# Attention times a gated MLP on one core: the sums of x are split behind the product that frees their home, stores of q and k go one product later, a quarter of x is reloaded ahead of W tile 10, and the first row tiles and V's last group are reordered

## The chip, the core and the metric

The kernel runs on one core of one Trainium2 chip. The core has five engines that take their instructions in order, each from a list of its own: TensorE (PE; its weight loads are listed apart as PEld and overlap it), VectorE (DVE), ScalarE (ACT), GpSimd (POOL) and SyncE (SP). They wait for one another through semaphores. In this kernel SyncE does nothing but issue DMA transfers; ScalarE issues some as well, and in the profile the DMA issues of these two stand apart as SPq and ACTq. Data lies in DRAM, in SBUF (where instructions take most operands) and in PSUM (where TensorE writes its products).

The metric is the time of one execution on the device, in microseconds (us). The profile is that of one execution, with times counted from the start of its span; the median of several executions is given beside it.

## The reference

With one batch, S = 2048 rows, D = 1024 columns, 32 heads of 32 columns and an MLP width of 3584:

```python
def _A_ref(x, wqkv, wo):
    qkv = (x @ wqkv).reshape(B, S, 3, H, Dh).transpose(2, 0, 3, 1, 4)
    q, k, v = qkv[0], qkv[1], qkv[2]
    scores = jnp.einsum("bhqd,bhkd->bhqk", q, k) * (Dh ** -0.5)
    p = _softmax(scores, axis=-1)
    o = jnp.einsum("bhqk,bhkd->bhqd", p, v)
    return o.transpose(0, 2, 1, 3).reshape(B, S, D) @ wo

def _B_ref(x, w1, b1, w2):
    h = jnp.einsum("bsd,df->bsf", x, w1) + b1
    act = h * jnp.tanh(softplus(h))          # mish
    return jnp.einsum("bsf,fd->bsd", act, w2)

xn = _layernorm(x, axis=-1)
return x + _A_ref(xn, wqkv, wo) * _silu(_B_ref(xn, w1, b1, w2))
```

## The kernel before, in words

**Arithmetic.** Almost every matrix product is taken with operands that are split in two: a high part, which ScalarE makes with a copy to the type fp32r, and a low part, which VectorE or GpSimd makes by subtracting the high part from the original (`copy`, L288, and `low`, L296). A product then takes three matmuls: high by high, and the two of high by low (`THREE`). A *split* below is one such copy with its subtraction.

**Four stages.** First comes the layernorm with the product for V, then the products for q and k, then attention and the MLP side by side, then the output projection. The columns of x are its 2048 rows turned round: four chunks of 512, each in SBUF as two units of four row blocks, `xc0_0` to `xc3_1`. Each unit holds a high and a low part, so it has four times [2 x 128 x 512].

**Layernorm and V.** A loop goes over 16 row tiles of 128 rows. For one tile, VectorE takes the statistics (`ln_a`, in three steps: two halves and their combination), ScalarE the inverse root (`ln_r`), VectorE the offsets (`ln_b`), ScalarE normalises (`ln_x`; for tiles 0 to 2, VectorE takes one half of it), TensorE transposes it (`ln_t`, tiles `pt`) and ScalarE and VectorE split the result into the units (`ln_c`). In the same turn `v_group(0, t - 2)` multiplies a row tile, two behind, with the first half of V's weights, 24 matmuls. These weights come in as `vraw` and are split into four buffers of two row blocks each, `vw0_0` to `vw0_3` (`v_high` and `v_low`, written out one by one for the first tiles, L470 to L495). The order of the 24 matmuls inside a group is a parameter: by default row block by row block with all three products each (`THREE`), otherwise two of the three products over all row blocks and then the third. When the last row tile is through, the second half of V's weights is split (`v_split(1, j)`) into the buffers that the first half leaves, and 16 more groups follow (`v_group(1, t)`).

During these last 16 groups, sums and differences of units of x are also formed (`t_half`), for the scheme of the next stage. Those for the chunk pair (0, 1) have no place in SBUF yet and are stored to DRAM, unsplit, as `ts0` to `ts3`, [128 x 512] at a time.

**q and k.** The columns of W for q and k are 8 column tiles each, and a column tile of q is paired with that of k; the sixteen "tiles" q = 0 to 15 are these 8 pairs for the chunk pair (2, 3) and then the same 8 for the pair (0, 1). A pair of column tiles times a pair of chunks is a 2 x 2 block product, made with seven products instead of eight, i = 0 to 6: A11, S2, A12, S3, S1, A22, S4, named by what W contributes. W's contribution is a block of W itself or a sum or difference of blocks (`w_sum`, on GpSimd), split by `piece(n)` into half of a buffer `wq{n // 2}`. x's contribution is a unit or a stored sum; the list `X` says which SBUF unit holds it, its *home*. `product(n)` issues 12 matmuls into a PSUM bank; then `after()` adds it to the others (`e` tiles, L777) or, when a block of q or k is complete, calls `out_`, which splits it into a staging tile `qst` (a ring of four) and stores that to DRAM through ScalarE's queue. `later.at(t, f)` does f t products later.

`SEQ` lists the products in order; some of tile 7 and tile 8 are moved between those of the tile before (`EARLY`). Counted from (7, 0), the first product of tile 7 to be issued, the index `since` means: 0 (7,0), 1 (6,1), 2 (6,2), 3 (7,2), 4 (6,3), 5 (6,4), 6 (7,1), 7 (6,5), 8 (6,6), 9 (7,3), 10 (7,4), 11 (8,0), 12 (7,5), 13 (7,6), 14 (8,1), and then 15 to 19 are (8,2) to (8,6). Pieces are made for two products at once: `wq26` holds those of (7,3) and (7,4), `wq27` those of (8,0) and (7,5).

At this passage from tile 7 to tile 8, x's contributions change. The sums for the pair (0, 1) have to come back from DRAM and be split into homes that the pair (2, 3) leaves: `xc2_0` is free after (7,0), `xc2_1` after (7,2), `xc3_0` after (7,1), `xc1_0` after (7,3). `t_load(i, k)` loads [128 x 512] of sum i into one of five small buffers and asks for its split three products later; odd k go to GpSimd, even k to VectorE. There are 16 such loads, in the order of sums 1, 2, 0, 3. The last unit, B22 (row blocks 4 to 7 of chunk 1), also comes back from DRAM, already split, into `xc1_1`, which is free after (7,4); it takes four loads of 512 KB and is first wanted by (8,6), since = 19. At the same time raw column tiles of W are loaded: each tile has two halves of 512 KB, a ring of two tiles serves up to tile 9 (`raw0` to `raw3`), and from tile 10 on two more stand in `spare`, the SBUF that `xc3_1` leaves after (7,6). All of these loads are issued by SyncE, in the order in which the code is written.

**Attention and MLP.** Here a planner (`Plan`) simulates the engines with estimated costs and due times and writes the order of all instructions. The score product `t` of head 0 needs, in two rows of `qstack0`, the negated row maxima; those of the last four row tiles of head 0 are made by `m_chain(0, 12, 4, ...)`: a reduction, a split, a transposition by TensorE (`mtp0_12`), a copy to `mt0_12` by ScalarE and two small DMAs into `qstack0` (`r6`), issued by SyncE.

## Time and profile before

| | us |
|---|---|
| three runs | 3372.64, 3367.37, 3369.28 |
| their median | 3369.28 |
| the profiled execution | 3371.32 |
| its span | 3369.5 |
| TensorE busy in the span | 3344.0 |
| VectorE busy | 2510.7 |
| ScalarE busy | 2056.4 |
| GpSimd busy | 2526.6 |

The mean clock granted to TensorE in the span is 0.999 of full speed. TensorE takes its first product of q and k at 202 us and its last at 530 us; attention and the MLP fill most of the rest.

How to read the rows of the profile. A row of busy times gives microseconds, the share of the span and the number of instructions. A row of waits gives the engine, operation, output tile and code line, `<-` what it waited for, and then the total in us, the number of waits and the longest. A row of a timeline gives the start, the duration of the group (several instructions of one kind that follow each other), the engine, the code line, the operation, output `<-` inputs, shapes, the count, and in brackets the idle time ahead of it and what ended it. A row of windows gives a stretch of time A:B, its length, then the busy time of TensorE (with the number of its matmuls), of its weight loads, of VectorE, ScalarE and GpSimd, then TensorE's granted clock, the busy share of the 16 DMA engines and the GB/s that they moved; where nothing ran on an engine its column is empty. Engine names with a q are DMA issues. Tile numbers are left out in these rows, so that `xc<-t` stands for the split of any sum into any unit.

### The profile page before, as it was taken

What the parts mean: (1) busy time and instruction counts of PE and PEld (TensorE: products, weight loads), DVE (VectorE), ACT (ScalarE), POOL (GpSimd) and SP (SyncE); (2) the same over time, 40 slices, a digit from 0 to 9 for tenths busy, and PEclk for the clock granted to TensorE, in tenths of its full rate; (3) what the DMA queues carried; (4) which work ended last, traced back from release to release, by engine and by line L of the source; (5) the groups of instructions that cost most, each with busy time, mean ns of one, the idle gap of its engine ahead of it and who ended that gap; (6) DMA issues with size and microseconds to landing.
All of it is one profiled execution on the core that took longest, in us unless ns stands there. A gap on an engine that the chain in (4) does not pass through costs nothing.

```text
span 3369.5 us, 45748 instructions
## 1 busy us (share of the span) xinstructions
PE 3344.0 (99%) x16867; PEld 2455.6 (73%) x16867; DVE 2510.7 (75%) x3984; ACT 2056.4 (61%) x3314; POOL 2526.6 (75%) x751
## 2 busy tenths in 40 slices
PE   8999999999999999999999999999999999999999
PEld 7888787777777777777677767777677777767787
DVE  6665677878777777887788778888787888886542
ACT  5233335777766666676676766767667766667621
POOL 2332445999999977888888988888888898889800
PEclk9999999999999999999999999999999999999999
DMA  7864755455555643334335434333344433433482
GB/s 242 297 207 165 238 163 166 149 176 161 166 175 179 210 135 114 113 117 118 112 113 156 136 101 126 100 102 113 113 151 132 123 101 111 127 114 107 137 305 84
DMA packets 291460, 501.56 MB, mean 149 GB/s; under 512 B 88138, under 2 KB 151114, under 8 KB 269130
## 3 DMA queue, kind: packets, MB, share of 16 engines
q1 hardware_dynamic: 271524, 456.95, 43.6%
q10 hardware_dynamic: 19712, 41.69, 3.3%
q8 instruction: 133, 2.18, 0.3%
q14 instruction: 91, 0.75, 0.1%
HBM read 352.55 MB, written 144.97 MB: 148 GB/s over the span
## 4 chain that ended last, share of the span: by engine, by line
PE 87%; DMA 2%; DVE 1%; ACT 0%; issue 0%; SPq 0%; ACTq 0%; POOL 0%; DVEq 0%
PE y L1290 18%; PE h L1200 18%; PE t L995 14%; PE s L913 13%; PE pv L1042 13%; PE op L1389 5%; PE q_y L792 2%; PE q_x L792 1%; PE q_z L792 1%; PE zp L1068 1%; PE s L697 0%; DMA xc<-xs 0%; DMA raw<-in_A_wqkv_dram 0%; DMA qstack<-mt 0%; DMA w2r<-in_B_w_dram 0%
## 5 line engine op out<-in xcount | busy, mean ns | idle before, releaser
L1024 POOL TENSOR_TENSOR z<-z,p 128x2048 f32<-128x2048 f32 x448 | 2067.9, 4616 | 97.4 <-ACT p L285 72.3
L285 ACT ACTIVATE p<-t,zero 128x512 f32<-128x512 f32 x2048 | 1376.9, 690 | 559.6 <-PE t L995 535.4
L919 DVE TENSOR_REDUCE mx<-s 128x1 f32<-128x512 f32 x1984 | 1322.3, 685 | 383.1 <-PE s L913 372.1
L1290 PE MATMUL y<-w,act 128*128 128x512 f32 x2688 | 920.7, 391 | 0.8 <-DVE yacc L1312 0.5
L995 PE MATMUL t<-qstack,kstack 128*128 128x512 f32 x2048 | 799.0, 393 | 3.3 <-DMA qstack<-mt 2.3
L913 PE MATMUL s<-kstack,qstack 128*128 128x512 f32 x1984 | 772.5, 393 | 0.0
L1200 PE MATMUL h<-xr,w 128*128 128x512 f32 x2016 | 697.7, 391 | 0.2 <-DMA xr<-xs 0.2
L1290 PEld LDWEIGHTS y<-w,act 128*128 128x128 f32 x2688 | 503.3, 188 | 114.5 <-issue 6.7
L995 PEld LDWEIGHTS t<-qstack,kstack 128*128 128x128 f32 x2048 | 383.8, 188 | 118.0 <-issue 20.1
L1042 PE MATMUL pv<-p,v 128*32 128x512 f32 x4096 | 459.3, 594 | 0.0
L913 PEld LDWEIGHTS s<-kstack,qstack 128*128 128x128 f32 x1984 | 369.7, 188 | 118.0 <-issue 32.1
L1200 PEld LDWEIGHTS h<-xr,w 128*128 128x128 f32 x2016 | 378.3, 188 | 80.9 <-issue 3.4
L1312 DVE TENSOR_TENSOR yacc<-yacc,y 128x512 f32<-128x512 f32 x416 | 282.7, 680 | 82.3 <-PE y L1290 81.2
L1042 PEld LDWEIGHTS pv<-p,v 128*32 128x32 f32 x4096 | 123.3, 110 | 282.9 <-issue 281.2
L1024 POOL TENSOR_TENSOR z<-p,p 128x2048 f32<-128x2048 f32 x32 | 148.0, 4626 | 185.6 <-PE zp L1068 136.1
L1200 PE MATMUL h<-xc,w 128*128 128x512 f32 x672 | 231.3, 391 | 0.3 <-ACT p L285 0.3
L354 PE MATMUL v<-vw,xc 128*128 128x512 f32 x768 | 180.3, 393 | 0.9 <-DVE vw L296 0.7
L354 PEld LDWEIGHTS v<-vw,xc 128*128 128x128 f32 x768 | 143.1, 189 | 31.9 <-DVE vw L296 1.8
L1200 PEld LDWEIGHTS h<-xc,w 128*128 128x128 f32 x672 | 125.9, 188 | 29.3 <-issue 2.5
L288 ACT ACTIVATE act<-h 128x512 fp32r<-128x512 f32 x112 | 66.6, 595 | 87.2 <-DVE h L1249 86.0
L792 PE MATMUL q_y<-xc,wq 128*128 128x512 f32 x480 | 115.4, 389 | 0.5 <-DVE e L777 0.5
L792 PEld LDWEIGHTS q_y<-xc,wq 128*128 128x128 f32 x480 | 90.0, 188 | 19.7 <-ACT wq L288 0.9
(146 smaller groups left out, 2943.5 us busy)
## 6 DMA issues: line engine op xcount, KB each, us to landing
w<-w1s SPq DMA_DIRECT2D x91, 1024.0 KB
w<-w2s SPq DMA_DIRECT2D x168, 512.0 KB
w2s<-w SPq DMA_DIRECT2D x56, 512.0 KB
qstack<-qs SPq DMA_DIRECT2D x96, 256.0 KB
kstack<-ks SPq DMA_DIRECT2D x96, 256.0 KB
w1s<-w SPq DMA_DIRECT2D x21, 1024.0 KB
qs<-qst ACTq DMA_DIRECT2D x32, 512.0 KB
ks<-qst ACTq DMA_DIRECT2D x32, 512.0 KB
```

What stands on the lines that cost most here:

```text
L285: nc.scalar.activation(out_, in_, fn, bias=zero if bias is None else bias, scale=scale)
L354: nc.tensor.matmul(ps, xc[t // 4][k // HK][:, a, k % HK, (t % 4) * P:(t % 4 + 1) * P], vw[i, k // 2][:, b, k % 2], start=n == 0, stop=n == ...
L792: nc.tensor.matmul(ps, w[:, a, k], xx[:, b, k], start=m == 0 and i in (0, 1, 4), stop=m == 3 * HK - 1, skip_group_check=i not in (0, 1, 4))
L913: nc.tensor.matmul(sp_, qst[h % 3][:, qt * P:(qt + 1) * P], kst[h % 3][:, kc * 512:(kc + 1) * 512], start=True, stop=True)
L919: nc.vector.reduce_max(tiles["mx"][:, qt, kc:kc + 1], tiles[qt, kc], axis=AX.X)
L995: nc.tensor.matmul(tp, kst[h % 3][:, kt * P:(kt + 1) * P], qst[h % 3][:, c * 512:(c + 1) * 512], start=True, stop=True)
L1024: nc.gpsimd.tensor_tensor(zs[h], pts[T - 1] if kt == 1 else zs[h], pts[T], ALU.add)
L1042: nc.tensor.matmul(pv[h][c * DH:(c + 1) * DH, :], vt[h][:, k, :], pts[T - kt + k][:, c * 512:(c + 1) * 512], start=k == 0, stop=k == NT - 1)
L1200: nc.tensor.matmul(t["h"], w1t[n][:, a, k], xts_[c][k // HK][:, b, k % HK], start=i == 0, stop=i == 3 * KT - 1)
L1290: nc.tensor.matmul(t["y"], acts[n][:, p, s * P:(s + 1) * P], w2t[m_][:, q], start=j == 0 and i == 0, stop=j == YB - 1 and i == 2)
L1312: nc.vector.tensor_tensor(ya, ya, t["y"], ALU.add)
L1389: nc.tensor.matmul(ps[t, dh], ohl[t // 4, k][:, a, s * P:(s + 1) * P], wt[k][:, b, r], start=k == 0 and i == 0, stop=k == KT - 1 and i == 2)
```

## The change

It has six parts.

1. In the first row tiles, the second and third step of tile 1's statistics move ahead of the subtraction for row block 2 of V's weights, on VectorE.
2. V's last group of the first half (row tile 15) takes its matmuls row block by row block, all three products of one before the next, instead of two products over all row blocks and then the third.
3. The splits of x's sums are no longer tied to three products behind their load. They stand in a list, and `T_SPLITS` takes two from it at since = 1, 2, 4, 5, 7, 8, 10 and 11, which is the product behind the one that frees the home, or the second behind it. `T_LOADS` starts the loads at since = -2 instead of 0 and ends them at 8 instead of 11.
4. B22's four loads are issued in two pairs at since = 11 and 12 instead of one each at 12 to 15, and the two halves of W tile 9 at 6 and 9 instead of 9 and 11.
5. The store of a block of q or k comes four products after the one that completed it instead of three.
6. The two small DMAs of head 0's last row maxima are issued by ScalarE instead of SyncE.

```diff
@@ first row tiles
     ln_a(1, (0,))
     ln_c(0)
+    ln_a(1, (1, 2))
     v_low(0, 2, nc.vector)
     v_high(0, 3)
     v_low(0, 3, nc.vector)
     for k in (4, 5):
         v_high(0, k)
         v_low(0, k, nc.gpsimd)
-    ln_a(1, (1, 2))
@@ the loop over row tiles
         evac = v_group(0, t - 2, {2: 22, 3: 20, 4: 14}.get(t, 8), (lambda: ln_t(t - 1)) if t <= NT else None,
-                       (((0, 0), (1, 0)), ((0, 1),)) if t == 2 else (((0, 0), (0, 1)), ((1, 0),)))
+                       (((0, 0), (1, 0)), ((0, 1),)) if t == 2 else None if t > NT else (((0, 0), (0, 1)), ((1, 0),)))
@@ q and k
+    t_splits = []
+
     def t_load(i, k):
...
-        later.at(3, split)
+        t_splits.append(split)
...
-    T_COUNT = (2, 1, 1) * 4
-    B_COUNT = {12: (0,), 13: (1,), 14: (2,), 15: (3,)}
+    T_LOADS = {-2: 3, -1: 1, 0: 1, 1: 2, 2: 2, 4: 2, 5: 2, 7: 2, 8: 1}
+    T_SPLITS = {s: 2 for s in (1, 2, 4, 5, 7, 8, 10, 11)}
+    B_LOADS = {11: (0, 1), 12: (2, 3)}
...
-        later.at(3, lambda: move(dst, st, nc.scalar))
+        later.at(4, lambda: move(dst, st, nc.scalar))
...
         later.tick()
+        since = n - SEQ.index((KT - 1, 0))
+        for _ in range(T_SPLITS.get(since, 0)):
+            t_splits.pop(0)()
...
         after()
-        since = n - SEQ.index((KT - 1, 0))
-        if 0 <= since < len(T_COUNT):
-            for _ in range(T_COUNT[since]):
-                t_load(*T_ORDER.pop(0))
-        if since in (9, 11):
-            q_load(9, ring_of(9), (since == 11,))
-        for k in B_COUNT.get(since, ()):
+        for _ in range(T_LOADS.get(since, 0)):
+            t_load(*T_ORDER.pop(0))
+        if since in (6, 9):
+            q_load(9, ring_of(9), (since == 9,))
+        for k in B_LOADS.get(since, ()):
             move(X[1][6][:, :, k], xs[1][:, :, HK + k])
@@ m_chain
         def r6(at):
             for a in range(2):
                 move(qst[h % 3][96 + a:97 + a, first * P:(first + n) * P]
-                     .rearrange("o (t p) -> o t p", p=P), tiles["mt"][n * a:n * a + n, :])
+                     .rearrange("o (t p) -> o t p", p=P), tiles["mt"][n * a:n * a + n, :], None if h else nc.scalar)
```

The order of TensorE's instructions is that of before but for V's last group. The other engines' lists change at these places. In the rows, tiles carry a number that tells allocations apart.

SyncE's list at the passage from tile 7 to tile 8, before. `t3_*` are the last loads of x's sums, `raw2` and `raw3` the two halves of W tile 9, `xc1_1` is B22's home, and `spare` holds W tile 10.

```order
L745 DMA t3_0_3005<-ts3_139 128x512
L745 DMA t3_1_3007<-ts3_139 128x512
L543 DMA raw2_1897<-in_A_wqkv_dram 128x8x128
L745 DMA t3_2_3029<-ts3_139 128x512
L745 DMA t3_3_3057<-ts3_139 128x512
L543 DMA raw3_1898<-in_A_wqkv_dram 128x8x128
L292 DMA xc1_1_186<-xs1_141 128x2x512
L543 DMA spare_3095<-in_A_wqkv_dram 128x8x128
L292 DMA xc1_1_186<-xs1_141 128x2x512 x2
L543 DMA spare_3095<-in_A_wqkv_dram 128x8x128
L292 DMA xc1_1_186<-xs1_141 128x2x512
L543 DMA spare_3095<-in_A_wqkv_dram 128x8x128
```

The same place in SyncE's list after:

```order
L747 DMA t0_3_2918<-ts0_136 128x512
L747 DMA t3_0_2920<-ts3_139 128x512
L543 DMA raw2_1897<-in_A_wqkv_dram 128x8x128
L747 DMA t3_1_2969<-ts3_139 128x512
L747 DMA t3_2_2971<-ts3_139 128x512
L747 DMA t3_3_2992<-ts3_139 128x512
L543 DMA raw3_1898<-in_A_wqkv_dram 128x8x128
L292 DMA xc1_1_186<-xs1_141 128x2x512 x4
L543 DMA spare_3102<-in_A_wqkv_dram 128x8x128 x3
L292 DMA zeros_156<-qstack0_3308 32x2048
```

The four loads of B22 now stand in one block behind `raw3`, and the three halves of W tiles in `spare` behind them.

VectorE's list between the additions e7_1 and e7_3 (of the products (7,1) and (7,3)), before. `wq26` and `wq27` are the W buffers described above, a row `xc<-t` is the subtraction of a sum's split, `qst` that of a block of q or k for the store, and the rows of L777 add products.

```order
L777 TENSOR_TENSOR e7_1_2924<-q7_y_2905,e7_0_2779 128x512
L296 TENSOR_TENSOR wq26_2942<-ws3_2891,wq26_2942 128x512
L296 TENSOR_TENSOR wq26_2942<-ws4_2838,wq26_2942 128x512
L296 TENSOR_TENSOR xc2_1_188<-t2_2_2872,xc2_1_188 128x512
L296 TENSOR_TENSOR qst6_1_3_2902<-e6_3_2870,qst6_1_3_2902 128x512
L777 TENSOR_TENSOR q6_y_2785<-q6_y_2785,e6_0_2762 128x512
L777 TENSOR_TENSOR q6_z_2874<-q6_z_2874,e6_1_2804 128x512
L296 TENSOR_TENSOR wq27_2990<-raw0_1895,wq27_2990 128x512
L569 SCALAR_TENSOR_TENSOR wq27_2990<-raw3_1898,wq27_2990 128x512
L296 TENSOR_TENSOR xc3_0_189<-t0_0_2926,xc3_0_189 128x512
L296 TENSOR_TENSOR qst6_1_2_2955<-q6_y_2785,qst6_1_2_2955 128x512
L777 TENSOR_TENSOR e7_3_3003<-q7_y_2905,e7_0_2779 128x512
```

The same place after:

```order
L780 TENSOR_TENSOR e7_1_2937<-q7_y_2922,e7_0_2786 128x512
L296 TENSOR_TENSOR wq26_2952<-ws3_2905,wq26_2952 128x512
L296 TENSOR_TENSOR wq26_2952<-ws4_2856,wq26_2952 128x512
L296 TENSOR_TENSOR qst6_1_3_2917<-e6_3_2882,qst6_1_3_2917 128x512
L296 TENSOR_TENSOR xc3_0_189<-t0_0_2839,xc3_0_189 128x512
L780 TENSOR_TENSOR q6_y_2790<-q6_y_2790,e6_0_2767 128x512
L296 TENSOR_TENSOR xc3_0_189<-t0_2_2886,xc3_0_189 128x512
L780 TENSOR_TENSOR q6_z_2888<-q6_z_2888,e6_1_2813 128x512
L296 TENSOR_TENSOR wq27_3006<-raw0_1895,wq27_3006 128x512
L569 SCALAR_TENSOR_TENSOR wq27_3006<-raw3_1898,wq27_3006 128x512
L296 TENSOR_TENSOR qst6_1_2_2968<-q6_y_2790,qst6_1_2_2968 128x512
L780 TENSOR_TENSOR e7_3_3016<-q7_y_2922,e7_0_2786 128x512
```

Two subtractions of sum 0, `t0_0` and `t0_2`, now stand ahead of the split of `wq27`; before, one of sum 2 did, and one of sum 0 stood behind it.

ScalarE's list at the end of q and k before: `p0` and `p1` are the exponentials of the first score products, `hl` the copy for the split of the row maxima, `mt0_12` the transposed ones.

```order
L285 ACTIVATE p0_4492<-t0_2_4499,zero_160 128x512
L288 ACTIVATE hl_3317<-nm0_12_4502 128x4
L288 ACTIVATE mt0_12_4525<-mtp0_12_4521 8x128
L285 ACTIVATE p0_4492<-t0_3_4551,zero_160 128x512
L285 ACTIVATE p1_4563<-t1_0_4556,zero_160 128x512
```

After, two DMA issues stand in it:

```order
L285 ACTIVATE p0_4492<-t0_2_4499,zero_160 128x512
L288 ACTIVATE hl_3316<-nm0_12_4502 128x4
L288 ACTIVATE mt0_12_4525<-mtp0_12_4521 8x128
L292 DMA qstack0_3308<-mt0_12_4525 1x4x128 x2
L285 ACTIVATE p0_4492<-t0_3_4551,zero_160 128x512
L285 ACTIVATE p1_4563<-t1_0_4556,zero_160 128x512
```

They stand directly behind the copy that makes their data, and ahead of the exponential of `t0_3`.

## The prediction

> **What bounds the kernel now.** I read the page's busy times first, then TensorE's waits, then its timeline at each wait, and last the queues of the engines named there.
>
> ```profile
> span 3369.5 us, 45748 instructions
> PE 3344.0 (99%) x16867; PEld 2455.6 (73%) x16867; DVE 2510.7 (75%) x3984; ACT 2056.4 (61%) x3314; POOL 2526.6 (75%) x751
> PE pt L423 <- ACT x L285: 9.8, 2, 9.0
> PE q_z L792 <- DMA xc<-xs: 3.3, 1, 3.3
> PE t L995 <- DMA qstack<-mt: 2.3, 2, 1.7
> PE q_y L792 <- DVE e L777: 1.9, 2, 1.4
> PE v L354 <- DVE vw L296: 0.7, 1, 0.7
> ```
>
> TensorE is busy for 3344.0 of 3369.5 us, so only 25.5 us can be won by moving work about, and 9.0 of them are the wait for the first tile of x. Every part of this change lies ahead of 545 us, and the order of TensorE's instructions behind that is the same in both kernels. TensorE alone sets the time there, so what is won or lost early should arrive at the end undiminished. The five wait rows are five places; the change touches all of them.
>
> The largest is where the projection passes from its first pair of chunks (q tiles 0 to 7) to its second.
>
> ```profile
> 319.36:349.29 29.93, 29.93 (x134) 24.78 (x133) 17.88 (x25) 13.96 (x26) 15.52 (x11) 1.00 0.69 229
> 349.29:388.00 38.71, 33.54 (x134) 26.41 (x133) 25.86 (x35) 15.71 (x29) 14.59 (x11) 0.91 0.78 258
> 349.29 2.88 PE L792 MATMUL q_x<-xc,wq 128*128 128x512 f32 x12
> 353.58 3.00 PE L792 MATMUL q_y<-xr,wq 128*128 128x512 f32 x12 [1.41 <-DVE e L777]
> 361.86 2.98 PE L792 MATMUL q_x<-xc,wq 128*128 128x512 f32 x12
> 365.34 2.98 PE L792 MATMUL q_y<-xc,wq 128*128 128x512 f32 x12 [0.50 <-DVE e L777]
> 373.60 2.20 PE L792 MATMUL q_z<-xc,wq 128*128 128x512 f32 x9
> 379.06 1.65 PE L792 MATMUL q_z<-xc,wq 128*128 128x512 f32 x3 [3.26 <-DMA xc<-xs]
> 380.50 4.89 PE L792 MATMUL q_x<-xc,wq 128*128 128x512 f32 x12
> 379.00:385.00 6.00, 5.94 (x15) 0.52 0.17 62
> ```
>
> The first two rows hold 134 matmuls each, eleven products of 2.72 us (29.93 / 11); the second eleven take 38.71 us, which is 8.8 more. From 349.29 to 353.58 is 4.29 (1.6 over), from 361.86 to 365.34 is 3.48 (0.8 over). The remaining 6.4 belong to one event: 3.26 us of waiting for the last quarter of B22, and then, as the last row shows, a clock of 0.52, at which twelve matmuls took 4.89 instead of 2.88.
>
> **B22 ahead of W tile 10.** The loads stand on SyncE's queue.
>
> ```profile
> 356.06 3.21 SPq L292 DMA_DIRECT2D xc<-xs  x1
> 364.37 5.32 SPq L292 DMA_DIRECT2D xc<-xs  x1
> 364.37 14.64 DMA xc<-xs
> ```
>
> Before, the four loads are issued from 356.06 to 369.7 with three of W tile 10 between them, and the last lands 14.64 us after 364.37, at 379.0. After, the four stand together ahead of W tile 10. What they still follow on SyncE is the second half of W tile 9, whose buffer comes free when VectorE has split the W piece of product (7,5), the second half of wq27 (in the rows below the split at 348.75; about 352 in the reckoning there). So they are issued from 352 to 354, W tile 9 and B22 being 2.5 MB. At the 258 GB/s of the second row, half of it left to the stores on ScalarE's queue, that is 19 us; at the whole rate 10. They land between 362 and 371. B22's last quarter is wanted at 375.8 before (373.60 + 2.20), hence at about 371.5 once the delays ahead of it are taken out. The wait goes, and with it the slow clock: minus 6.4. Bounds: minus 6.4, and minus 3.2 if 19 us is right and the clock falls all the same. What is late next is VectorE.
>
> **The sums of x, and the stores.** VectorE was 25.86 us busy in the slow stretch against 17.88 ahead of it, and its lateness explains the waits of 1.41 and 0.50.
>
> ```profile
> 341.69 1.79 DVE L296 TENSOR_TENSOR wq<-ws,wq 128x512 fp32r<-128x512 f32 x2
> 343.56 1.67 POOL L551 TENSOR_TENSOR ws<-raw 128x512 f32<-128x512 f32 x1 [1.23 <-DVE wq L296]
> 345.70 0.68 DVE L777 TENSOR_TENSOR q_y<-q_y,e 128x512 f32<-128x512 f32 x1
> 346.27 0.63 ACT L288 ACTIVATE xc<-t 128x512 fp32r<-128x512 f32 x1 [4.01 <-issue]
> 347.94 0.89 DVE L296 TENSOR_TENSOR wq<-raw,wq 128x512 fp32r<-128x512 f32 x1 [0.95 <-ACT wq L288]
> 348.75 1.78 DVE L569 SCALAR_TENSOR_TENSOR wq<-raw,wq 128x512 fp32r<-128x512 f32 x1
> 352.76 0.67 DVE L777 TENSOR_TENSOR e<-q_y,e 128x512 f32<-128x512 f32 x1
> ```
>
> A VectorE operation with both inputs in SBUF takes 0.89 by itself (347.94) and up to 1.78 beside GpSimd; one that reads PSUM keeps 0.68 (345.70). The two take turns, some 1.7 us for one of each. The change does not remove any of the 16 splits (a copy on ScalarE, a subtraction on VectorE or GpSimd); it moves them two or three products earlier. The first four now fall at 324 to 328, where VectorE and GpSimd had been idle. The order rows say what then happens at 341 to 352: between e7_1 and e7_3 there stand ten operations on VectorE before and ten after, but after, two subtractions of x's sums (t0_0, t0_2) lie ahead of the split of wq27, where before one did (t2_2). I follow the queues by these durations, in turns wherever GpSimd has work: e7_1 ends at 341.3, wq26 is split by 343.2, qst6_1_3 by 343.9, t0_0 by 345.6, q_y by 346.2. ScalarE can then copy qst6_1_2, t0_2, t0_3 and both pieces of wq27 by 349.1, which lets VectorE do t0_2 by 348.6, q_z by 349.2, the first piece of wq27 by 350.3, the second by 352.0 and e7_3 by 353.2. TensorE wants the first of these pieces at its third matmul behind 349.29, at 349.75, and waits 0.6; it then wants e7_3 at 352.6 and waits 0.7. So I keep 1.3 of stall here and win 2.4 (1.6 and 0.8) minus 1.3, about 1.0. Bounds: 2.4 if turns are kinder, and a loss of 1.0 if they are harsher by one pair (1.7) at each of the two places. The second wait (0.50, at 365) goes, since two fewer subtractions are left by then.
>
> Stores a product later: no instruction more. ScalarE sat idle for 4.01 before 346.27 because a store in its queue waited for qst<-e; that block goes, but what stood behind it waited for q_y at 345.70 anyway, so it is worth 0.4 to VectorE and is in the reckoning above. In the other tiles of W TensorE shows no wait, and I cost it at nothing there; the cover is a staging ring of four, reused seven products later.
>
> **V's last group.**
>
> ```profile
> 104.69 13.72 PE L354 MATMUL v<-vw,xc 128*128 128x512 f32 x59
> 112.70 3.24 ACT L288 ACTIVATE vw<-vraw 128x512 fp32r<-128x512 f32 x6 [3.48 <-PE v L354]
> 119.13 33.09 PE L354 MATMUL v<-vw,xc 128*128 128x512 f32 x143 [0.72 <-DVE vw L296]
> ```
>
> The group of row tile 15 starts 16 matmuls (3.6 us) into the first row, at 108.3. Before, it reads its first W buffer until matmul 18 (112.4), and ScalarE's splits start at 112.70. After, it has done with it at matmul 6, 109.7: the splits start 2.7 us earlier, and the wait of 0.72 goes. Minus 0.7.
>
> **The first row tiles.**
>
> ```profile
> 12.24 2.39 DVE L296 TENSOR_TENSOR vw<-vraw,vw 128x512 fp32r<-128x512 f32 x2
> 12.72 3.07 POOL L296 TENSOR_TENSOR vw<-vraw,vw 128x512 fp32r<-128x512 f32 x2 [11.42 <-ACT vw L288]
> 15.59 0.74 DVE L296 TENSOR_TENSOR vw<-vraw,vw 128x512 fp32r<-128x512 f32 x1
> 18.06 1.10 PE L423 MATMUL pt<-ident_r,x 128*128 128x128 f32 x8 [0.85 <-ACT x L285]
> ```
>
> The statistics of tile 1 move ahead of two subtractions on VectorE, but its normalisation stays behind these and a third. VectorE has no idle time there. Before, the first of the three starts at 12.24 and is nearly through when GpSimd begins at 12.72, and the third ends at 16.3 (15.59 + 0.74). After, the first starts behind 12.72 too, so one more of 0.74 takes its turn between there and the end, which becomes 17.1. Normalising, and TensorE at 18.06, come later by up to 0.8; I take plus 0.6, bounds 0.8 and minus 0.3 (the statistics' own 1.0 less what overlaps).
>
> [...]
>
> **The row maxima of head 0 on ScalarE's queue.**
>
> ```profile
> 533.04 0.37 ACTq L292 DMA_DIRECT2D qs<-qst  x1
> 536.30 1.21 SPq L292 DMA_DIRECT2D qstack<-mt  x2
> 540.67 0.47 PE L995 MATMUL t<-qstack,kstack 128*128 128x512 f32 x1 [1.66 <-DMA qstack<-mt]
> DMA  8999999798996999999998889999996200000464
> ```
>
> The last row cuts 525 to 545 into slices of half a microsecond: the DMA engines are full until 540.5. The two small transfers gain nothing at their issue, since they follow ScalarE's copy in both kernels. But on ScalarE's queue they now stand behind the last stores of q and k, which themselves go later: one more store of 512 KB is still to be moved. At 305 to 410 GB/s (what the slices moved) that is 1.3 to 1.7 us. I take plus 1.2. Bounds: minus 0.4 if it makes no difference whose queue it is and SyncE's issue is saved, plus 4.6 if 1.7 makes the wait 3.3 long and the clock falls as it did after 3.26 (2.9 more: 6.4 minus 3.26, rounded down).
>
> [...]
>
> **Sum.** Minus 6.4, minus 1.0, minus 0.7, plus 0.6, plus 1.2: minus 6.3. The profiled execution took 3371.32 us, so 3365.0; the median of the three runs, 3369.28, is 2.0 below it, so 3363.0. A measurement of this kernel tells about 0.2% from no change, 6.7 us: the borders are 3362.5 and 3376.0, and the forecast lies next to the first.
>
> **Rivals.**
> *Everything goes clean* (0.23): VectorE is in time, the maxima are not delayed, the front neither. Minus 6.4, 2.4 and 0.7: minus 9.5, 3359.8. For it: the first four splits fall into idle time. Against: 16 splits and GpSimd's sums still share 30 us.
> *A slow clock in a new place* (0.20): one of the waits at 352 or 541 grows past 3.2 us, and 2.9 come back: minus 3.4, 3365.9. For it: 3.26 was enough at 376; the wait at 541 is reckoned at 2.9. Against: 1.66 and 1.41 were not.
> *B22 is hardly earlier* (0.08): it still waits for W tile 9's buffer; if VectorE frees that after 355, half of the 6.4 stays: minus 3.1, 3366.2.
> *Slower* (0.10): the 16 loads share five buffers, so a load waits for a split five earlier, and ScalarE, which takes its queue in order, holds back evacuations behind a copy whose load has not landed.
>
> ```profile
> 353.15 1.89 SPq L745 DMA_DIRECT2D t<-ts  x2
> 361.50 0.63 ACT L288 ACTIVATE xc<-t 128x512 fp32r<-128x512 f32 x1 [2.00 <-DMA t<-ts]
> ```
>
> A load here took 8.3 us. Copy, subtraction and issue add 2.4, so three rounds from 324 end at 356, in time for the product at 368. It decides from landings of about 12.5 us: then the rounds end behind 368. At the 14.64 of the B22 load they end at 375, TensorE stands 7 us and more behind (plus 2.9 for the clock twice), and B22's gain is lost with them: some 3378. Against it: the first loads are issued before the DMA engines are full (share 0.69 in the first stretch).
>
> **The numbers.** The forecast has 0.39, between minus 4.5 and minus 8; a third of it (0.14) lies beyond 6.7. Faster: 0.23 + 0.14 = 0.37. Slower: 0.10. Same: 0.53. The range leaves out the slower case and the very best: 3358 to 3369. The forecast alone: 3361 to 3365.
>
> **What would show it.** Right: no wait for xc<-xs and no clock of 0.5 between 340 and 400; B22's issues in one block near 352; waits of about half a microsecond on W pieces or e near 350; the group at 119 without a wait; transposes of tile 1 at 18.6; the wait for qstack<-mt between 2.5 and 3.3. Wrong: a wait above 3 us anywhere in 320 to 400, or xc<-t copies on ScalarE that wait for t<-ts.

## The result, and the profile after

The changed kernel took 3365.27 us (median of 22 runs, 3362.9 to 3367.08) and the kernel before, in 22 runs beside it, 3370.52 us (3367.37 to 3373.51). The ratio is 0.9984 with a 95% interval of 0.9977 to 0.9990. So the change takes 5.25 us off, clear of the noise, but less than the 6.7 us from which on the prediction would have called it faster; in its terms this is "same", to which it gave 0.53. The forecast was 3363.0, which is 6.3 below the 3369.28 from which it started. The profiled execution took 3366.45 us, 4.9 less than the one before. Medians here and below leave out two executions, one of `b22_late` (5648 us) and one of `store3` (6918 us), whose granted clock was 0.56 on the average of the span.

The page and the waits of TensorE, after:

```profile
span 3364.7 us, 45751 instructions
PE 3342.9 (99%) x16867; PEld 2455.6 (73%) x16867; DVE 2511.9 (75%) x3984; ACT 2056.0 (61%) x3314; POOL 2527.5 (75%) x751
PE t L999 <- DMA qstack<-mt: 3.3, 2, 2.5
PE h L1204 <- DMA xr<-xs: 0.4, 1, 0.4
PE q_y L795 <- DVE e L780: 0.4, 1, 0.4
PE q_x L795 <- DVE wq L296: 0.3, 1, 0.3
PE q_z L795 <- DVE e L780: 0.3, 1, 0.3
```

The wait for xc<-xs (B22, 3.3 us) is gone and so is the one in V (0.7). The waits for e, 1.9 together, have become 0.4 and 0.3 on a W piece. The last row is a new wait, at 218 us, in the first products of q and k. The wait for the row maxima has grown from 2.3 to 3.3.

TensorE executes the same 16867 matmuls in the same order in both kernels (inside V's last group the order differs, the number doesn't), so the n-th start of one trace can be set against the n-th of the other. The lead is the difference; minus is earlier than before.

| place (time before) | lead | step | forecast of the step |
|---|---|---|---|
| transposes of tile 1 (18 us) | +0.35 | +0.35 | +0.6 |
| behind V's last group (130) | -1.15 | -1.50 | -0.7 |
| behind the first products of q and k (226) | -0.67 | +0.48 | 0 |
| product (8,6), ahead of B22 (373.6) | -1.85 | -1.18 | -1.0 |
| one product later (385.5) | -8.04 | -6.19 | -6.4 |
| ahead of the row maxima (538.6) | -7.90 | +0.14 | 0 |
| some matmuls behind them (545.3) | -5.74 | +2.16 | +1.2 |
| the end | -4.86 | +0.88 | 0 |

TensorE's timeline at the passage from tile 7 to tile 8, after, and then SyncE's:

```profile
349.62 2.56 PE L795 MATMUL q_x<-xc,wq 128*128 128x512 f32 x10 [0.34 <-DVE wq L296]
352.61 2.98 PE L795 MATMUL q_y<-xr,wq 128*128 128x512 f32 x12 [0.43 <-DVE e L780]
371.75 2.88 PE L795 MATMUL q_z<-xc,wq 128*128 128x512 f32 x12
374.47 2.88 PE L795 MATMUL q_x<-xc,wq 128*128 128x512 f32 x12
...
351.29 0.38 SPq L543 DMA_DIRECT2D raw<-in_A_wqkv_dram  x1
351.77 3.21 SPq L292 DMA_DIRECT2D xc<-xs  x4
```

The two short waits are at the places where 0.6 and 0.7 were reckoned. Product (8,6), at 371.75, runs through without a stop, and the next takes 2.88 us where it took 4.89. B22's four loads begin at 351.77, directly behind the second half of W tile 9; by the DMA records they land from 358.9 to 364.6.

TensorE's timeline at the front, at V's last group and at the row maxima, after, and last a window of 2 us behind the maxima:

```profile
8.95 1.97 PE L423 MATMUL pt<-ident_r,x 128*128 128x128 f32 x8 [8.95 <-ACT x L285]
18.41 1.10 PE L423 MATMUL pt<-ident_r,x 128*128 128x128 f32 x8 [0.58 <-ACT x L285]
105.00 21.36 PE L354 MATMUL v<-vw,xc 128*128 128x512 f32 x93
533.58 0.77 PE L999 MATMUL t<-qstack,kstack 128*128 128x512 f32 x1 [2.47 <-DMA qstack<-mt]
...
533.00:535.00 2.00, 1.42 (x3) 1.16 (x4) 0.18 (x1) 0.61 (x1) 0.00 (x0) 0.52 0.05 18
```

From 105.00 there are 93 matmuls without a wait. The wait for the maxima is 2.47 us long, and behind it the granted clock is 0.52.

### The profile page after: what moved, and what is told of

Same layout as the page of the kernel before. It is cut to its first block, busy times and chain, and to the rows that moved or that the text cites. A ratio compares the mean times of both kernels' runs of the same rounds, so it can differ in the third digit from the quotient of the medians.

```text
span 3364.7 us, 45751 instructions
## 1 busy us (share of the span) xinstructions
PE 3342.9 (99%) x16867; PEld 2455.6 (73%) x16867; DVE 2511.9 (75%) x3984; ACT 2056.0 (61%) x3314; POOL 2527.5 (75%) x751
## 4 chain that ended last, share of the span: by engine, by line
PE 95%; DMA 2%; DVE 1%; POOL 1%; issue 0%; ACT 0%; SPq 0%; ACTq 0%; DVEq 0%; POOLq 0%
PE y L1294 18%; PE h L1204 17%; PE t L999 14%; PE s L917 13%; PE pv L1046 13%; PE op L1393 5%; PE v L354 5%; PE q_y L795 3%; PE q_z L795 2%; PE q_x L795 2%; PE zp L1072 1%; POOL z L1028 1%; DMA raw<-in_A_wqkv_dram 0%; PE pt L423 0%; PE s L697 0%
```

## The experiments

Every kernel was timed beside the kernel before; "less" is its median minus that of the kernel before on the same chip. The change itself has -5.25 there, and -6.40 in a repetition (`again`, below), so differences of about 1 us between such numbers tell little; the leads in the traces are finer. They are gathered here, for the same places as above (that at 130 is told behind the table):

| kernel | 18 | 226 | 373.6 | 385.5 | 538.6 | 545.3 | end | less |
|---|---|---|---|---|---|---|---|---|
| the change | 0.35 | -0.67 | -1.85 | -8.04 | -7.90 | -5.74 | -4.86 | -5.25 |
| `b22_late` | 0.50 | -0.70 | -1.87 | -7.85 | -7.91 | -6.83 | -5.59 | -5.52 |
| `b22_alone` | 0.38 | 0.38 | 0.39 | -5.81 | -5.86 | -5.56 | -3.42 | -4.98 |
| `splits_late` | 0.27 | -0.72 | -1.59 | -7.78 | -7.81 | -5.11 | -3.45 | -5.06 |
| `sums_b22_late` | 0.64 | 0.04 | -0.51 | -2.76 | -2.46 | -1.77 | 0.21 | -1.17 |
| `mt_sync` | 0.31 | -0.89 | -2.12 | -8.32 | -8.32 | -7.38 | -6.19 | -5.69 |
| `store3` | 0.70 | -0.14 | -1.36 | -7.56 | -7.61 | -7.24 | -6.86 | -6.71 |
| `mt_sync_store3` | 0.49 | -1.01 | -2.23 | -8.43 | -8.48 | -8.33 | -7.41 | -6.54 |
| `v_after_mt` | 0.44 | -0.86 | -2.04 | -8.23 | -8.28 | -5.11 | -3.83 | -5.01 |
| `front_old` | -0.26 | -1.11 | -2.33 | -8.53 | -8.38 | -7.38 | -5.61 | -7.02 |
| `combo` | -0.55 | -1.90 | -3.10 | -9.30 | -9.36 | -7.52 | -6.73 | -7.97 |
| `combo_v` | -0.07 | -0.73 | -1.91 | -8.11 | -8.15 | -7.72 | -7.21 | -8.47 |
| `again` | 0.48 | -0.38 | -1.56 | -7.75 | -7.54 | -5.12 | -0.72 | -6.40 |

The column 226 holds two things. At V's last group, between 107 and 130 us, the lead moves by -1.47 in each of the twelve traces that have the new order, and by nothing in `b22_alone`, which has the old one and its wait. At 218 us, up to 0.9 of this is lost again, a different amount in each trace (0.5 in the change, nothing in `mt_sync_store3`); a wait for e stands there. What sets that amount is not shown.

### Which edit removed the wait for B22

The prediction gave the 6.4 us to one edit, B22's loads ahead of W tile 10. Four kernels take this and the earlier loads of x's sums apart. First, `b22_late`:

```diff
-    B_LOADS = {11: (0, 1), 12: (2, 3)}
+    B_LOADS = {12: (0,), 13: (1,), 14: (2,), 15: (3,)}
...
-        if since in (6, 9):
-            q_load(9, ring_of(9), (since == 9,))
+        if since in (9, 11):
+            q_load(9, ring_of(9), (since == 11,))
```

> The changed kernel with B22's four loads and W tile 9 back at their old places (since = 12 to 15, and 9 and 11), everything else changed. If the term of the sum for B22 is right and stands by itself, a wait of about 3 us for xc<-xs comes back near 372 us with a clock of about 0.5 behind it, and the time rises by 5 to 6.5 us. Rival: the earlier loads of x's sums were what made B22 early (the DMA engines are less busy by then), so the wait is under 1.5 us and the time rises by less than 2.

The rival had it. Without the edit that was to bring 6.4 us the lead at 385.5 is -7.85. SyncE's timeline, and TensorE's at (8,6):

```profile
358.75 1.24 SPq L292 DMA_DIRECT2D xc<-xs  x2
360.03 0.61 SPq L543 DMA_DIRECT2D spare<-in_A_wqkv_dram  x1
360.68 4.35 SPq L292 DMA_DIRECT2D xc<-xs  x1
...
371.73 3.08 PE L795 MATMUL q_z<-xc,wq 128*128 128x512 f32 x12
```

B22 still has loads of W tile 10 ahead of its last quarter, but the sums' loads, of which two were issued ahead of it as late as 353.15 in the kernel before, are out of the way by then. The issue of that quarter begins at 360.68, against 364.37 there. It comes just in time: (8,6) takes 3.08 in place of 2.88.

Next the opposite, `b22_alone`: that edit alone, put into the kernel before.

```diff
-    B_COUNT = {12: (0,), 13: (1,), 14: (2,), 15: (3,)}
+    B_COUNT = {11: (0, 1), 12: (2, 3)}
...
-        if since in (9, 11):
-            q_load(9, ring_of(9), (since == 11,))
+        if since in (6, 9):
+            q_load(9, ring_of(9), (since == 9,))
```

> The kernel before, with one part of the change alone: B22's four loads at since = 11 and 12 and the halves of W tile 9 at 6 and 9. Theory C (either edit brings B22's last load forward on SyncE's queue, and one is enough): no wait for xc<-xs near 375 us, full clock there, and the waits for e near 353 and 365 stay (1.4 and 0.5); the time falls by 6 to 7 us. Theory D (only the earlier loads and splits of the sums of x cure it, the new place of B22's loads is worth nothing): the wait for xc<-xs stays above 2 us and the time falls by less than 2 us.

And `splits_late`: the change with the sums back.

```diff
-        t_splits.append(split)
+        later.at(3, split)
...
-    T_LOADS = {-2: 3, -1: 1, 0: 1, 1: 2, 2: 2, 4: 2, 5: 2, 7: 2, 8: 1}
-    T_SPLITS = {s: 2 for s in (1, 2, 4, 5, 7, 8, 10, 11)}
+    T_LOADS = dict(enumerate((2, 1, 1) * 4))
+    T_SPLITS = {}
```

> The changed kernel with the loads and splits of x's sums back at their old places (loads from since = 0 to 11, each split three products behind its load). Theory C: no wait for xc<-xs, but the waits for e of 1.4 and 0.5 us come back in place of 0.34 and 0.43, so the time rises by about 1 us (0.8 to 1.5). Theory D: a wait for xc<-xs of 2 to 3.3 us comes back and the time rises by 3 to 7 us.

Then `sums_b22_late`, the change with the edits of `b22_late` and `splits_late` together.

> The changed kernel with both undone: the sums' loads and splits, and B22's loads and W tile 9, back at their old places; the later stores, V's last group, the first row tiles and the maxima on ScalarE's queue stay. Theories C and D both: the wait for xc<-xs comes back at about 3.3 us and the waits for e with it, and the time rises by 5 to 8 us, to that of the kernel before within 2 us. If the later stores had cured it (theory E), it would not come back. A clock near 0.5 behind the wait would say that it belongs to a wait of this length; full clock, that it is chance.

Timelines of SyncE and TensorE, first of `b22_alone`:

```profile
355.51 5.88 SPq L292 DMA_DIRECT2D xc<-xs  x4
353.96 2.98 PE L792 MATMUL q_y<-xr,wq 128*128 128x512 f32 x12 [1.39 <-DVE e L777]
365.74 2.97 PE L792 MATMUL q_y<-xc,wq 128*128 128x512 f32 x12 [0.53 <-DVE e L777]
373.99 2.88 PE L792 MATMUL q_z<-xc,wq 128*128 128x512 f32 x12
376.71 2.88 PE L792 MATMUL q_x<-xc,wq 128*128 128x512 f32 x12
```

Of `splits_late`:

```profile
353.53 5.92 SPq L292 DMA_DIRECT2D xc<-xs  x4
352.63 3.00 PE L795 MATMUL q_y<-xr,wq 128*128 128x512 f32 x12 [1.16 <-DVE e L780]
372.01 2.88 PE L795 MATMUL q_z<-xc,wq 128*128 128x512 f32 x12
```

And of `sums_b22_late`:

```profile
360.22 3.25 SPq L292 DMA_DIRECT2D xc<-xs  x2
364.22 0.37 SPq L543 DMA_DIRECT2D spare<-in_A_wqkv_dram  x1
364.64 4.06 SPq L292 DMA_DIRECT2D xc<-xs  x1
377.34 1.48 PE L795 MATMUL q_z<-xc,wq 128*128 128x512 f32 x3 [2.05 <-DMA xc<-xs]
378.62 4.01 PE L795 MATMUL q_x<-xc,wq 128*128 128x512 f32 x12
```

Theory C stands and D and E fall. Either edit alone removes the whole wait; only with both undone does it come back (2.05 us, where 3.3 was expected, and the product behind it 4.01 us instead of 2.88), and then the time is that of the kernel before (ratio 0.9999, 0.9989 to 1.0008). What decides is when the last of the four loads leaves SyncE's queue: at 364.37 and 364.64 in the two kernels that wait, at 360.88 or earlier in the four that don't. From there to its last packet it takes 11.4 us in `b22_late` and 11.5 in `sums_b22_late`, so the 4 us between these two arise in the queue and not in the transfer. Either the sums can be moved out of its way, or W tile 10 together with W tile 9; the two halves of this second edit were not tried apart. In `b22_alone` the step at B22 is 0.39 to -5.81, minus 6.2, and the other waits stay what they were (1.39, 0.53).

The term for VectorE behaves alike. Its waits at 350 to 365 cost 1.18 us less in the change (from -0.67 to -1.85); with the sums back but stores late 0.87 (`splits_late`) or 0.55 (`sums_b22_late`) of that stay, with stores back but sums early (`store3`) 1.22 stay, and only in `b22_alone`, which has neither, does nothing stay. The wait at 365 did not come back in `splits_late`, so its time rose by less than the 1 us expected (0.2 by the last column).

### What lengthened the wait for the row maxima

`mt_sync`:

```diff
-                     ..., tiles["mt"][n * a:n * a + n, :], None if h else nc.scalar)
+                     ..., tiles["mt"][n * a:n * a + n, :])
```

> The changed kernel with one part undone: SyncE issues the two small DMAs of head 0's last row maxima again. Theory A (they are held up behind the last stores of q and k in ScalarE's queue): TensorE's wait for qstack<-mt falls from 2.47 to 1.7 us or less, as before the change, the clock stays full behind it, and the time falls by about 2 us (0.8 of wait and 1.3 of slow clock). Theory B (the DMA engines share their time among all queues, so that the maxima arrive when the last store does, whoever issues them): the wait stays between 2.2 and 2.6, the slow clock too, and the time is within 0.5 us of that of the change.

Its queues, TensorE's timeline and the same window:

```profile
528.00 1.25 SPq L292 DMA_DIRECT2D qstack<-mt  x2
533.27 0.47 PE L999 MATMUL t<-qstack,kstack 128*128 128x512 f32 x1 [2.58 <-DMA qstack<-mt]
533.00:535.00 2.00, 1.73 (x8) 1.45 (x9) 0.99 (x2) 1.23 (x2) 0.00 (x0) 1.00 0.01 3
```

The wait is no shorter when SyncE issues the transfers: 2.58. Theory A falls. Only the slow clock, which B had as well, is missing. `store3`:

```diff
-        later.at(4, lambda: move(dst, st, nc.scalar))
+        later.at(3, lambda: move(dst, st, nc.scalar))
```

> The changed kernel with the stores of q and k back at three products behind the product instead of four. Theory A (queue): one store fewer stands ahead of the maxima; the wait for qstack<-mt falls by 0.5 to 1.3 us and the slow clock with it, in all 1.5 to 2.5 us off the time, unless ScalarE, blocked by a store that waits for its low part, delays the passage from tile 7 to tile 8: then a wait of 0.3 to 0.8 us for e or wq comes back near 350 and the gain is that much smaller. Theory B (backlog): the same at the maxima, since the backlog is smaller by the same store.

And `mt_sync_store3`, the two edits together:

> The changed kernel with both undone. If queue and stores act apart (theory A), the wait for qstack<-mt is 1.66 us as before the change, or less, without a slow clock, and the time lies 2 to 3 us below that of the change. If only the backlog counts (theory B), it equals the kernel with the stores alone undone to 0.5 us.

TensorE's timeline in these two, `store3` first:

```profile
533.43 0.47 PE L999 MATMUL t<-qstack,kstack 128*128 128x512 f32 x1 [2.02 <-DMA qstack<-mt]
```

```profile
532.34 0.47 PE L999 MATMUL t<-qstack,kstack 128*128 128x512 f32 x1 [1.80 <-DMA qstack<-mt]
```

With the earlier stores the wait is 2.02 (ScalarE issues) and 1.80 (SyncE), with the later ones 2.47 and 2.58. From the first issue to TensorE's start it is 4.70 and 4.49 against 5.14 and 5.27. So the later stores cost 0.4 to 0.8 us, and the queue 0.2 one way or 0.1 the other, which is nothing. All the traces bear this out: the wait is 1.66 to 2.11 in the six with stores at three products, and 2.36 to 2.75 in the seven with stores at four and V's load in its place. The two pairs do not vary the queue alone, though: when ScalarE issues the maxima, SyncE's next load (w2r, 256 KB) goes 3 to 5 us ahead of them (525.37 in the change, 523.77 in `store3`), otherwise behind them (529.30, 529.12). Of the last four stores the first two go 9.7 and 4.8 us ahead of the maxima in the change (518.74 and 523.67 to 528.44), and 12.1 and 5.8 ahead in `store3` (516.61 and 522.96 to 528.73); the last two stand alike. In all four kernels TensorE starts 0.2 to 0.7 us behind the last store's last packet. The queue's only visible trace is that the two issues take 1.80 us on ScalarE and 1.25 on SyncE.

The prediction took it that the maxima come behind the stores because both stand in ScalarE's queue. In `mt_sync` they have SyncE's queue to themselves: the last packet of the load w<-w1s ahead of them came at 528.6, as the second of them was issued. Had the queue been the reason, they should then have gone ahead of the stores. They didn't. By the DMA records their last packet came 3.7 us after the second issue, against 1.3 us for the same transfer at 479 us, where the engines were idle (busy share 0.01 from 479 to 480 in the change). Between 528.6 and 531.6 no packet of SyncE's queue is on record, while ScalarE's moved 1.2 MB.

`v_after_mt` was to take 256 KB of V in packets of 128 B out from in front of the maxima:

```diff
-            nc.sync.dma_start(vt[h], vs[h // 16][:, :, h % 16])
+            if h:
+                nc.sync.dma_start(vt[h], vs[h // 16][:, :, h % 16])
@@ r6, behind the two transfers
+            if h == 0 and first == 12:
+                nc.sync.dma_start(vt[0], vs[0][:, :, 0])
```

> The changed kernel, with one load moved: head 0's V (256 KB in 2048 packets of 128 B, 3 us of the DMA engines between 521 and 524 us) is issued by SyncE behind the small transfers of the row maxima instead of five microseconds ahead of them; its first user, pv, runs at 553 us. Theory B (the maxima arrive when the DMA engines have worked off what was issued ahead of them): the wait for qstack<-mt falls from 2.5 us to under 1 us, there is no slow clock behind it, and the time falls by 1.5 to 3 us. Theory F (the small transfers take this long by themselves: 4.4 to 5.1 us from issue to arrival): the wait stays above 2 us.

```profile
523.08 0.62 SPq L959 DMA_DIRECT2D v<-vs  x1
533.94 0.47 PE L1002 MATMUL t<-qstack,kstack 128*128 128x512 f32 x1 [3.21 <-DMA qstack<-mt]
```

The edit did not do what the expectation says. The maxima stand in ScalarE's queue and the load in SyncE's, which waits for nothing there, so V went at 523.08 instead of 516.96: not behind the maxima, but into the crowd ahead of them. The wait rose to 3.21. That speaks for B, though not by the route intended. It also shows turns: from 529 to 532 us, V's packets on SyncE's queue and those of the stores on ScalarE's alternate, 568 of the one and 532 of the other.

### The first row tiles

`front_old` puts the statistics back behind the subtractions:

```diff
     ln_c(0)
-    ln_a(1, (1, 2))
     v_low(0, 2, nc.vector)
...
         v_low(0, k, nc.gpsimd)
+    ln_a(1, (1, 2))
```

> The changed kernel with tile 1's statistics back behind the subtractions for V's weights. By the prediction's term the transposes of tile 1 begin 0.3 to 0.6 us earlier (18.06 to 18.1 us in place of 18.4) and everything behind them too; at the end this is lost among the runs' differences: 0 to -0.6 us. Rival: the shift at the front is not this edit's but varies from one execution to the next, and the transposes begin at 18.4 or later.

```profile
8.73 1.97 PE L423 MATMUL pt<-ident_r,x 128*128 128x128 f32 x8 [8.73 <-ACT x L285]
17.80 1.10 PE L423 MATMUL pt<-ident_r,x 128*128 128x128 f32 x8 [0.54 <-ACT x L285]
```

Both are right in part. The first transposes begin anywhere from 8.15 to 9.38 us in these traces, whatever the kernel. From them to the transposes of tile 1 it takes 9.46 (18.41 - 8.95) with the new order, 9.45 to 9.48 in all the kernels that have it, and 9.07 (17.80 - 8.73) with the old, as before (18.06 - 9.00); of the others with the old order, `b22_alone` and `combo_v` have 9.07 and 9.05, and only `combo` 9.36, where VectorE waited 0.5 us for the load of tile 1's x. The edit costs 0.4 us. It is lost at the subtractions for V's weights: the three take 3.57 us on VectorE in the change, where the first two run beside GpSimd's, and 2.38 and 0.74 in `front_old`. That is the sign and about the size of the prediction's term (0.4 for the 0.6 taken).

### A better version

`combo` leaves the new places of the loads and V's last group, and has the edits of `front_old`, `store3` and `mt_sync` together. `combo_v` adds that of `v_after_mt`, so that V's load now stands behind the maxima in the same queue.

> What the runs so far favour: the new places of the sums' and B22's loads and V's last group stay, the statistics of tile 1, the stores (three products) and the maxima (SyncE) go back. From the parts: 0.4 us at the front and 0.8 at the wait for qstack<-mt (1.8 us) against the change, in all 1 to 1.5 us below it without a slow clock, 2 to 3 with one: about 3363 to 3364.5 us beside a change of 3365.3. If the terms do not add, it equals the change to 0.5 us.

> The same, and head 0's V loaded behind the maxima. Theory B: the wait for qstack<-mt is under 0.5 us, and the time lies 1 to 2 us below that of the kernel without this (about 3362). Theory F: no difference between the two. A wait for v or an earlier one for xr<-xs that eats the gain would show as a wait behind 545 us.

Their ratios are 0.9975 (0.9965 to 0.9984) and 0.9975 (0.9966 to 0.9985), medians 3364.6 and 3364.1 beside 3372.57 before. That is 1.6 to 3.2 us better than the change, by the last column of the table, but the intervals overlap. In the traces `combo` is ahead by 9.36 us at 538.6, in a favourable execution that began at 8.15. V's load was not what held the maxima up: with it out of the way `combo_v` waits 2.11, `combo` 1.88, so the expectation of under 0.5 was wrong; in `combo` that load's last packet came at 522.2, before the last two stores were issued (522.94 and 523.71). TensorE's timeline of `combo` at the maxima, and three windows:

```profile
531.53 0.47 PE L999 MATMUL t<-qstack,kstack 128*128 128x512 f32 x1 [1.88 <-DMA qstack<-mt]
...
531.00:533.00 2.00, 1.47 (x7) 1.24 (x8) 0.73 (x2) 0.96 (x2) 0.00 (x0) 1.00 0.08 28
533.00:535.00 2.00, 2.00 (x6) 1.61 (x5) 1.61 (x3) 1.09 (x3) 0.00 (x0) 0.51 0.00 0
535.00:537.00 2.00, 2.00 (x7) 1.53 (x6) 1.41 (x3) 2.00 (x4) 0.82 (x1) 0.64 0.62 213
```

Here the clock falls after a wait of only 1.88, and only once TensorE has run at full clock for more than a microsecond.

### The change once more

`again` is the changed kernel without any edit.

> The changed kernel itself once more, to see what of its trace is chance. What belongs to the kernel returns to 0.2 us: 9.46 us from the first transposes to those of tile 1, no wait in V's last group, waits of 0.34 and 0.43 near 350, no wait for xc<-xs, a wait for qstack<-mt of 2.3 to 2.8. If the slow clock behind that wait (0.52 in the first trace) belongs to the wait's length, it returns; if it is chance, as full clock behind 2.6 and 2.7 us in three other kernels suggests, it may not, and the wait for xr<-xs at 2511 us (0.4 there, 1.1 to 1.5 in most others) may change as well. Time: 3364 to 3367 us.

Ratio 0.9980 (0.9971 to 0.9989), median 3366.25, in the range expected. The short waits, the 9.47 us at the front and the 2.58 at the maxima return, and in this trace the slow clock does too. This execution (3370.59 us, the slowest of its eleven) lost 4.4 us from 545 us on, at waits of which the kernel before shows little or nothing. Two of them in TensorE's timeline:

```profile
1350.00 0.47 PE L999 MATMUL t<-qstack,kstack 128*128 128x512 f32 x1 [1.91 <-DMA qstack<-mt]
2515.79 0.50 PE L1204 MATMUL h<-xr,w 128*128 128x512 f32 x1 [0.89 <-DMA xr<-xs]
```

## Why the prediction was right, and where it was not

**The sum.** Of the 6.3 us forecast, 4.86 came in the profiled execution and 5.25 in the medians. Of the 2.3 us between 3363.0 and 3365.27, 1.2 lie in the start: the forecast was taken from the median of three runs, 3369.28, and the 22 runs beside the change have 3370.52. By the table, the terms miss by 1.0 at the row maxima, by 0.9 behind them and by 0.5 at 218 us, and V's last group makes up for 0.8 of it. That misses of both signs partly cancel is luck.

**B22.** The size was right: 6.4 forecast, 6.2 measured in the change and in `b22_alone`, half of it wait and half slow clock. The issue at 352 to 354 and the landing between 362 and 371 were near (351.8, and 358.9 to 364.6). Wrong was to give it to the one edit. The reckoning of SyncE's queue stopped at W tile 9 and did not ask what B22 would do with the sums' loads out of its way and nothing else moved: `b22_late` shows that this is enough, with 0.2 us lost. The rival "B22 is hardly earlier" had its condition, W tile 9's buffer later than 355, but the earlier loads of the sums would have covered part of that too, as they do in `b22_late`.

**The sums and the stores.** The two waits came where the queues of VectorE were followed to, at 0.34 and 0.43 for 0.6 and 0.7, and the step was 1.18 for 1.0. Stores a product later were given 0.4 in VectorE's reckoning. In fact they bring 0.55 by themselves (`sums_b22_late`), and with the earlier sums in place their own share is nothing (1.22 without them in `store3`). The 0.89 us at 347.94, given as that of a VectorE operation by itself, had one of GpSimd's beside it until 348.28; with none beside them the splits of W pieces take 0.68 to 0.69 in the kernel before. The turns are in its rows: from 348 to 352, operations of GpSimd and VectorE end in alternation, at 349.99, 350.53, 351.69 and 352.23, so 1.70 us for one of each.

**V's last group.** The wait went as forecast, and stands in the traces of `before` and `b22_alone` alone. The size was off: the term counted only the wait of the row, 0.72, but the step is 1.47 in every trace with the new order. The matmuls behind the wait came slower too, without a row of their own (twice 0.34 and once 0.44 us from one start to the next in place of 0.23). The prediction has no loss at 218 us, where 0.5 of it went again in the change.

**The first row tiles.** Plus 0.4 for 0.6; the mechanism, taking turns with GpSimd, fits: the third subtraction ended at 16.8, for 17.1 reckoned and 16.3 before.

**The row maxima.** The term was taken at plus 1.2 and measured 2.16 in the first trace. Its first half was near: the wait grew by 0.8. But the step of the prediction, "on ScalarE's queue they now stand behind the last stores", does not explain the wait. That the queue itself holds the maxima back was the author's estimate; no run shows it, and with SyncE's queue in its place the wait was 2.58 us for 2.47. Of the two reasons given only the other holds, the stores' delay, 0.4 to 0.8 us on either queue. The second half, 1.35 us of slow clock, had been allowed only past a wait of about 3.3; it came at 2.47. Whether it comes at such a wait is chance, as the last section shows. With it the rival "a slow clock in a new place" happened in part, at the place it named but without its condition, and the measured 3365.27 lies nearer to that rival's 3365.9 than to the forecast of 3363.0.

**The rest.** That what is won early "should arrive at the end undiminished" held up to 545 us outside the places in the table: from 226 to 348 us the leads change by less than 0.1, from 385.5 to 538.6 by 0.3 at most. From there to the end the change lost 0.88 us and the experiments 0.4 to 4.4. A good part of it is the wait for xr<-xs: 0.18 in the one trace of the kernel before, 0.44 to 1.5 in the others. It does not follow the lead: `sums_b22_late`, with none to speak of, has 1.4. `b22_alone`, the kernel before with only B22's and W tile 9's loads moved, has 1.36. Whether the change lengthens it, or that one trace was lucky, stays open.

**Slower.** The rounds of five buffers did not hold ScalarE back: in the change, no wait of TensorE between 320 and 400 was above 0.43.

## What to carry to other kernels

When a load is late, list everything that stands ahead of it in its queue and ask for each whether moving it would be enough; two edits that both free the queue are worth what one is, and undoing either alone shows next to nothing (here a lead of 7.85 and 7.78 us at 385.5 for 8.04, and 2.76 with both undone). In these traces a small transfer that TensorE waits for arrived about when the DMA engines had worked off the large ones issued ahead of it (at the row maxima its user started 0.2 to 0.7 us behind the last store's last packet, in the change and the three kernels with `mt_sync` and `store3`); so count the megabytes issued in the five microseconds before it, and don't count on another queue to help: here the wait was 2.58 us on SyncE's and 2.47 on ScalarE's. Setting the matmuls of two traces one against the other, in order, shows steps of half a microsecond that the times, with their spread of 4 us, can't; but set the places so that each step holds one cause, and compare several traces, since the step from 18 to 226 us, 0.6 to 1.5 in these traces, is a constant 1.47 and a varying loss behind it. A wait costs more than its row where the clock falls behind it, here by 1.35 to 1.62 us at the row maxima: look at how much idle time falls into one step of 3.413 us (below).

## What was not expected of the hardware

**The slow clock.** It does not go by the length of the wait alone. At the row maxima there are 14 traces with waits of 1.66 to 3.21 us. Behind five of them (1.88, 2.47, 2.58, 2.75, 3.21) the clock was half for 3.41 us, at a cost of 1.35 to 1.62; behind the others, up to 2.71, it stayed full, 2.58 among both.

What it goes by in these traces can be read from their records of the granted clock. In each of the 14, every switch stands a whole number of steps of 3.413 us behind the first rise, to 0.01 us. One can therefore cut each trace into such steps and add up TensorE's idle time in each, from 20 us to the last matmul. Seven steps at full clock have 1.88 us or more (1.88, 1.96, 2.05, 2.10, 2.28, 2.36, 2.75), and behind each of them the clock is half for the next step (in the kernel before, at B22, for two). All others have 1.80 or less, and behind none of them does it fall. The change's wait of 2.47 lay with 1.96 in one step; that of `mt_sync`, 2.58, was cut into 1.03 and 1.55 by the border of a step. So in these 14 traces the limit lies between 1.80 and 1.88 us of idle time in one step, and a wait of 1.9 to 2.7 us had a slow clock behind it or not by where it fell.

**An almost empty queue.** The two transfers of 2 KB took as long in SyncE's otherwise empty queue (`mt_sync`) as in the one that held the stores (the change), 5.27 against 5.14 us from the first issue to their user's start. They did not take part in the turns that `v_after_mt` shows between the two queues: their first packets came only when the stores were nearly through, 3.6 us after their issue, against 1.2 us for the same transfers at 479 us. What held them until then is not shown.
